# K and V of six batches as four rows on 128 partitions and a padded rest: linear attention and a gated MLP on one Trainium2 core

## The chip, the cores and the metric

The kernel runs on one core of one Trainium2 chip. The core has a matrix engine (TensorE; in the profile PE for matmuls and PEld for weight loads), a vector engine (VectorE, DVE), a scalar engine (ScalarE, ACT), a general engine (GpSimd, POOL) and a queue engine (SyncE, SP). Each takes its instructions in order. Here POOL issues the loads from memory, which also convert 32-bit to 16-bit floats, and SP issues the stores and the transposing transfers between tiles. The metric is device microseconds of one execution; lower is better.

## What is computed

Eight batches with eight heads each, 576 positions, 64 values per head. For each batch and head a 64x64 matrix is formed from K and V over all positions, Q is multiplied by it, and each row is normalized. The result, 4608 rows of 512, goes through two matrix products with a gate between them.

```python
def _attn_ref(q, k, v, g_norm) -> np.ndarray:
    kv = np.einsum('bhsd,bhse->bhde', k, v)
    out = np.einsum('bhsd,bhde->bhse', q, kv)
    rms = np.sqrt(np.mean(out * out, axis=-1, keepdims=True) + 1e-06)
    return (out / rms * g_norm).astype(np.float32)

def _moe_ref(x, w_in, w_out) -> np.ndarray:
    h = x @ w_in
    g = h * (1.0 / (1.0 + np.exp(-1.702 * h)))
    return (g @ w_out).astype(np.float32)
```

## The kernel before, in words

**Stages.** The loop over t (L925) has nine stages. Stage t puts 512 rows of batch t through the two products of the second half: the first with the gate (`hid_seven`, matmuls of L527; in stage 0 `first_columns` and L420), then the one with w_out (`Seven.run`, L647; in stage 0 `project_all`, L761). Stages 1 to 8 use seven products of half size in place of eight, with sums made on VectorE (xS, gS, ws and tw are such sums). The last stage takes the 64 remaining rows of each of the eight batches, gathered in `x_rem`.

**Attention runs one batch ahead.** In stage t the attention of batch t + 1 is put between the steps of the two products. The order is written by hand: `at1` and `at2` hang a piece of work behind a numbered step of the first or second product, and a Plan names the order of the first product's steps, "kv" among them. Instructions stand on each engine in the order in which the program makes them; semaphore waits between engines are added from the tiles that they read and write.

**K times V.** `kv(c)` handles a pair of heads. `kv_product` (L215) sums over positions: K is the weight and V the moving operand, 64 columns each, and the two heads of a pair write the two halves of the output partitions in turn. Positions lie as 96 partitions of six rows each (PE_ = 96, NJ = 6), so each head takes six matmuls, each pair 12, and each batch 48. Batch 0 runs them in stage 0's beginning, batch 1 in four pieces in the second half of stage 0 (steps 36, 37, 49 and 50), batches 2 to 7 in one piece of 48 at "kv" (`kv_all`). VectorE then copies the sum into kvb or kvd (L355, L477).

**Loads of K and V.** There is one buffer each, `kraw` and `vbuf`, so the loads of a batch wait until the product of the batch before has read them. `load_kv` (L107) makes one DMA for K and one for V, with 96 partitions and, per head, one run of six rows: 1536 bytes in memory. Batch 2 is loaded in stage 0 in two halves, behind steps 39 and 51; batch t + 2 is loaded in stage t behind "kv". On POOL's queue `load_q` follows (L116): q's first 512 positions as 128 partitions of four rows, 1024 bytes per run, and the 64 remaining ones as two DMAs into `qrem`, of 64 partitions and 256 bytes per run.

**What else uses the DMA engines.** Behind step 100 of stage t, SP transposes q of batch t + 2 into qTd and qTr (L242, L244). The normalized rows x of batch t + 1 are transposed into xT, which the next stage reads (`turn`, L316). SP also issues the stores of the results.

**Stage 0's end on VectorE.** Behind steps 49 to 62 stand the copies of batch 1's products, `apply` (L341), copies of the results (L770) and the first sums xS (L459) of stage 1.

Of the kernel before, what the change touches and what calls it, by code (L numbers as in the profile page):

```python
# [12 lines left out]
P = 128  # L13
# [3 lines left out]
def kernel(  # L17
# [10 lines left out]
    nc = tc.nc  # L28

    B, H, S, D = q.shape  # L30
    DM = H * D
    DFF = moe_w_in.shape[1]
    NPAIR = H // 2
# [3 lines left out]
    SM = 512  # L37
    J = SM // P
    R = S - SM
# [22 lines left out]
    srcs = {"k": k, "v": v, "q": q}  # L62
# [21 lines left out]
    raw = {"k": kraw, "q": qraw, "v": vbuf}  # L84

    def early_src(n, b, c0, c1):
        return srcs[n][b, 2 * c0 : 2 * c1].rearrange("h (p j) d -> p h (j d)", j=NJ)

    def early_load(n, b, c0, c1):
        nc.gpsimd.dma_start(  # L90
            out=raw[n][0:PE_, c0:c1, :].rearrange("p c (l x) -> p (c l) x", l=2),
            in_=early_src(n, b, c0, c1),
        )
# [10 lines left out]

    def load_kv(b, c0=0, c1=NPAIR):  # L107
        early_load("k", b, c0, c1)
        early_load("v", b, c0, c1)

    def q_rows(b):

# [16 lines left out]
    for n in "kqv":  # L129
# [11 lines left out]
        out=ident,  # L141
        in_=ident,
# [50 lines left out]
    class Attention:  # L193
        ss_pool = rest_pool = (ps_a, "att")
        KEEP = NPAIR

# [11 lines left out]
        def kv(self, c):  # L208
            if c % self.KEEP == 0:
                self.kvp = ps_a.tile([P, NPAIR, D], F32, name="kvp", tag="att")  # L210
            self.kv_product(self.kvp[:, c, :], c)
            if (c + 1) % self.KEEP == 0:
                self.keep_kv(c + 1 - self.KEEP, c + 1)

        def kv_product(self, t, c):  # L215
            for j in range(NJ):
                for hl in range(2):
                    x = slice((hl * NJ + j) * D, (hl * NJ + j + 1) * D)
                    nc.tensor.matmul(  # L219
                        t[hl * D : (hl + 1) * D, :],  # L220
                        kraw[0:PE_, c, x],
                        vbuf[0:PE_, c, x],
                        start=(j == 0),
                        stop=(j == NJ - 1),
                    )
# [6 lines left out]
        def keep_kv(self, c0, c1):  # L232

            for half in range(2):
                to = slice(half * D, (half + 1) * D)
                for hl in range(2):
                    r = slice(hl * D, (hl + 1) * D)
                    copy(self.engine, self.kb[to, c0:c1, half, 1 - hl], self.kvp[r, c0:c1, :])
# [109 lines left out]

    class Early(Attention):
        KEEP = 2  # L350

        def keep_kv(self, c0, c1):
            for hl in range(2):
# [370 lines left out]
    def layers(t, units1, units2):  # L724
        hid = d0 if t == 0 else Hidden(t)
        seven = Seven(t, hid.gT) if t else None
        left = hid_seven(t, hid, seven, units1) if t else first_columns(hid, units1)
        osbs[t] = opool.tile([P, 4, DM], F32, name="osb", tag="osb")
        if t:
            todo = {n: [lambda x=x: seven.sums(*x) for x in xs] for n, xs in plan(t).later.items()}  # L730
            for n, us in units2.items():
                todo.setdefault(n, []).extend(us)
            for n, us in left.items():
                todo[n] = us + todo.get(n, [])
            seven.run(todo)
        else:
            project_all(hid.gT, units2)
        if t < EARLY:
            store_early(t)
        elif t < B and t not in HALVED:  # L740
            store(t, 0, J)
# [174 lines left out]
    def plan(t):  # L916
        return SECOND if t < EARLY else LATER if t < B - 1 else LAST_TWO
# [7 lines left out]
    for t in range(NT):  # L925
        b = t + 1
        u1, u2 = {}, {}

        def at1(i, f, *args):
            u1.setdefault(i, []).append(lambda: f(*args))  # L930

        def at2(i, f, *args):
            u2.setdefault(i, []).append(lambda: f(*args))  # L933

        def of(b, name, *args):
            return lambda: getattr(live[b], name)(*args)

        if t == 0:
            for l in range(2):
                at1(6, nc.vector.memset, kvd[l], 0.0)  # L940
            at1(7, of(0, "out", NPAIR))
            at1(7, scale_w_in, 0, 4)
            at1(7, w_in_sums, 0, 2)
            at1(8, start, 1)
            at1(11, scale_w_in, 4, 6)
            at1(11, w_in_sums, 2, 3)
            at1(13, load_q, 2)
            at2(4, setattr, a0, "ss_pool", Attention.ss_pool)
            at2(4, of(0, "ss", NPAIR, True))
            at2(4, of(0, "apply", NPAIR))  # L950
            at2(18, weight_sum, 0, 0, HF)
            at2(18, scale_w_in, 6, 8)
            at2(18, w_in_sums, 3, 4)
            for c in range(NPAIR):
                at1(12, of(1, "pack_q", c))
                at2(9 + 3 * c, of(1, "q", c))
                at2((36, 37, 49, 50)[c], of(1, "kv", c))
                at2((41, 43, 54, 55)[c], of(1, "out", c))
                at2((45, 50, 58, 60)[c], of(1, "ss", c))
                at2((48, 52, 58, 62)[c], of(1, "apply", c))  # L960
            for n in range(1, 4):
                at2(19, weight_sum, n, 0, 4)
                at2(38, weight_sum, n, 4, 6)
            at2(39, load_kv, 2, 0, 2)
            at2(51, load_kv, 2, 2, NPAIR)

            def first_sum():
                made[1] = Sums(1, xT[1])
                made[1].form(0)

            at2(55, first_sum)
        elif b < B:
            todo = plan(t)
            at1(todo.steps.index("kv"), of(b, "kv_all", todo.keep))
            if t == 1:
                at1(5, start, b)
                at1(5, of(b, "transpose_q"))
                at1(4, nc.scalar.preload_act_table_set, "gelu_apprx_sigmoid_and_others")
                for n, i in ((1, 8), (2, 11), (3, 16)):
                    at1(i, weight_sum, n, 6, HF)  # L980
            if t + 2 < B:
                late = max(15, todo.steps.index("kv") + 1)
                at1(late, load_kv, t + 2)
                at1(late, load_q, t + 2)
                at2(100, start, t + 2)
                at2(100, of(t + 2, "transpose_q"))
            at = todo.attn
            at2(at["table"], nc.scalar.preload_act_table_set, "abs_reciprocal_sqrt_and_small")
            for h in range(2):
                at2(at["roots"][h], of(b, "roots", h))  # L990
            for j in range(J):
                for name in ("rows", "add_up", "turn"):
                    at2(at[name][j], of(b, name, j))
            at2(46, of(b, "out", NPAIR))
            at2(74, of(b, "ss", NPAIR))
            at2(80, of(b, "apply", NPAIR))
            at2(82, nc.scalar.preload_act_table_set, "gelu_apprx_sigmoid_and_others")
        elif t < B:
            for name in ("ss_pool", "rest_pool"):
                at2(16, setattr, live[1], name, (ps_a, "att"))  # L1000
            at2(16, of(1, "out", NPAIR))
            at2(34, nc.scalar.preload_act_table_set, "abs_reciprocal_sqrt_and_small")
            at2(44, of(1, "ss", NPAIR))
            at2(50, of(1, "apply", NPAIR))
            at2(52, nc.scalar.preload_act_table_set, "gelu_apprx_sigmoid_and_others")
        layers(t, u1, u2)
# [30 lines left out]
```

## Time and profile before

| | |
|---|---|
| median of three runs | 263.08 us (262.53 to 263.4) |
| the profiled execution | 262.59 us, span 260.8 us |
| TensorE busy | 252.9 us, 97% of the span, 2548 matmuls |
| TensorE weight loads busy | 207.0 us, 79% |
| VectorE busy | 194.2 us, 74% |
| ScalarE busy | 174.9 us, 67% |
| GpSimd busy | 44.1 us, 17% |
| granted TensorE clock | 1.0 throughout |
| loads issued by GpSimd | 28112 packets, 18.17 MB written |

The span reaches from the first to the last instruction; the rest of the execution's time lies around it. Matmuls are pipelined and their ends are modelled, so a busy TensorE says little by itself: the chain of work that ended last, and what TensorE waited for, say whether it is the bound. In the chain each row gives the start, the length, and the engine, tile and line, with the number of instructions merged. In the groups each row gives line, engine, operation, tiles, shapes and count, then the busy time and the mean duration of one, then the idle time before. In the rows of DMA issues the last number is the time from issue to landing, and KB are those written. In the stretches each engine's busy time is followed, in the single rows, by the instructions in brackets.

### The profile page before, as it was taken

The numbers are of one execution on the slowest core, as the hardware profiler recorded it, in microseconds if no ns is written. First come the engines' busy times: TensorE is split into PE (matmuls) and PEld (weight loads), VectorE is DVE, ScalarE is ACT, GpSimd is POOL, SyncE is SP. The second block draws the span as 40 slices with busy tenths as digits, with TensorE's granted clock in tenths as the row PEclk, the third lists the DMA queues.
The fourth block names the chain that finished last, engine by engine and source line by source line (L and its number), as shares of the span: only waits on it lengthen the run. The fifth ranks groups of instructions, "written<-read, shape, count | busy, mean of one in ns | idle before, by whom it ended". The sixth has DMA issues, their size and how long they took to land.

```text
span 260.8 us, 6238 instructions
## 1 busy us (share of the span) xinstructions
PE 252.9 (97%) x2548; PEld 207.0 (79%) x2548; DVE 194.2 (74%) x349; ACT 174.9 (67%) x315; POOL 44.1 (17%) x69
## 2 busy tenths in 40 slices
PE   7899999999999999999999999999999999999993
PEld 2444544788888988898889888998899888888882
DVE  1566676899968986899689958995899587466941
ACT  3477724988639963996399648974797569737810
POOL 8872234004023002300140004000000000000001
PEclk9999999999999999999999999999999999999999
DMA  7999999979979946995699369946600510021005
GB/s 175 194 202 205 205 204 197 246 162 144 190 153 189 203 71 161 117 240 78 159 150 234 53 158 149 237 54 155 155 1 13 157 77 0 3 101 63 1 3 161
DMA packets 59311, 35.33 MB, mean 135 GB/s; under 512 B 31570, under 2 KB 56658, under 8 KB 59154
## 3 DMA queue, kind: packets, MB, share of 16 engines
q0 software_dynamic: 28112, 18.17, 49.6%
q1 hardware_dynamic: 30768, 16.36, 26.2%
q8 instruction: 20, 0.33, 0.5%
q10 hardware_dynamic: 402, 0.39, 0.5%
q14 instruction: 9, 0.07, 0.1%
HBM read 36.70 MB, written 9.44 MB: 177 GB/s over the span
## 4 chain that ended last, share of the span: by engine, by line
PE 89%; DMA 6%; POOL 2%; issue 0%; DVE 0%
PE h L527 38%; PE o L647 38%; PE o L761 5%; DMA w_in_sb<-in_moe_w_in_dram 4%; PE kvp L219 2%; DMA qraw<-in_q_dram 2%; PE outR L279 2%; PE hT L420 2%; POOL w_in_sb L154 2%; PE ss L327 1%; PE q L401 0%; PE outT L252 0%; PE outT L256 0%; POOL vbuf L90 0%; DVE osb L627 0%
## 5 line engine op out<-in xcount | busy, mean ns | idle before, releaser
L507 ACT ACTIVATE gT<-h 128x512 f16<-128x512 f32 x96 | 52.7, 604 | 5.4 <-PE h L527 5.3
L527 PEld LDWEIGHTS <-ws 128*128 128x128 f16 x512 | 50.1, 98 | 5.9
L647 PEld LDWEIGHTS <-gS 128*128 128x128 f16 x512 | 49.7, 98 | 5.6
L527 PE MATMUL h<-xS,ws 128*128 128x256 f16 x384 | 52.2, 272 | 0.0
L647 PE MATMUL o<-tw,gS 128*128 128x256 f16 x384 | 46.3, 273 | 0.0
L527 PEld LDWEIGHTS <-w_in_sb 128*128 128x128 f16 x384 | 37.1, 98 | 4.7
L647 PEld LDWEIGHTS <-gT 128*128 128x128 f16 x384 | 37.0, 98 | 4.0
L647 PE MATMUL o<-w_out_sb,gT 128*128 128x256 f16 x256 | 33.5, 273 | 0.0
L527 PE MATMUL h<-xT,w_in_sb 128*128 128x256 f16 x224 | 31.9, 273 | 0.0
L541 DVE TENSOR_TENSOR h<-h,s 128x512 f32<-128x512 f32 x32 | 22.2, 698 | 7.7 <-PE h L527 5.9
L624 DVE TENSOR_TENSOR osb<-o,qf 128x512 f32<-128x512 f32 (+1 forms) x25 | 16.7, 668 | 15.0 <-PE o L647 12.3
L90 POOL DMA_DIRECT2D kraw<-in_k_dram x12 | 8.7, 724 | 103.9 <-PE kvp L219 101.4
L543 DVE TENSOR_TENSOR s<-h,s 128x512 f32<-128x512 f32 x32 | 22.1, 691 | 3.9 <-PE h L527 3.1
L579 DVE TENSOR_TENSOR gS<-gT 128x512 f16<-128x512 f16 (+2 forms) x32 | 21.6, 684 | 0.7 <-ACT gT L507 0.7
L507 ACT ACTIVATE gT<-s 128x512 f16<-128x512 f32 x32 | 19.8, 628 | 2.7 <-DVE s L543 2.6
L329 ACT ACTIVATE rs<-ss,eps_t 128x512 f32<-128x512 f32 (+1 forms) x16 | 9.2, 582 | 16.8 <-PE ss L327 16.7
L527 PE MATMUL h<-xS,w_in_sb 128*128 128x256 f16 x128 | 18.9, 273 | 0.0
L933 ACT ACT_TABLE_LOAD x14 | 18.0, 1283 | 0.3
L680 POOL DMA_DIRECT2D out_dram<-osb x2 | 1.1, 564 | 94.2 <-DVE osb L624 94.2
L477 ACT COPY h<-h 128x512 f32<-128x512 f32 x27 | 15.6, 585 | 2.1 <-PE h L527 2.0
L477 ACT COPY s<-h 128x512 f32<-128x512 f32 x18 | 10.6, 588 | 9.5 <-PE h L527 8.8
L527 PE MATMUL h<-xT,ws 128*128 128x256 f16 x112 | 16.8, 273 | 0.0
(92 smaller groups left out, 362.4 us busy)
## 6 DMA issues: line engine op xcount, KB each, us to landing
out_dram<-osb SPq DMA_DIRECT2D x10, 512.0 KB, 3.1
kraw<-in_k_dram POOLq DMA_DIRECT2D x5, 576.0 KB, 8.4
vbuf<-in_v_dram POOLq DMA_DIRECT2D x5, 576.0 KB, 11.6
qraw<-in_q_dram POOLq DMA_DIRECT2D x3, 512.0 KB, 13.5
qbuf<-in_q_dram POOLq DMA_DIRECT2D x3, 512.0 KB, 14.6
kraw<-in_k_dram POOLq DMA_DIRECT2D x4, 288.0 KB, 10.4
vbuf<-in_v_dram POOLq DMA_DIRECT2D x4, 288.0 KB, 10.6
out_dram<-osb SPq DMA_DIRECT2D x6, 192.0 KB, 5.0
```

The source lines that it names most:

```text
L90: nc.gpsimd.dma_start(out=raw[n][0:PE_, c0:c1, :].rearrange("p c (l x) -> p (c l) x", l=2), in_=early_src(n, b, c0, c1),)
L329: nc.scalar.activation(rs[:, 0:n], t[:, 0:n], AFT.Abs_reciprocal_sqrt, bias=eps_t, scale=1.0 / D)
L477: (nc.vector.tensor_copy if engine == "D" else nc.scalar.copy)(to, src)
L507: nc.scalar.activation(self.gT[:, to, n * TH : (n + 1) * TH], src, AFT.Gelu_apprx_sigmoid)
L527: nc.tensor.matmul(bank[name][:, a], w, x, start=(p in (1, 5) and a == 0 and k == 0), stop=(k == KH - 1), skip_group_check=True,)
L541: nc.vector.tensor_add(bank["z"], bank["x"], self.s5)
L543: nc.vector.tensor_add(self.s5, bank["x"], self.s5)
L579: op(s[:, n, lo], a, b)
L624: nc.vector.tensor_add(o, ps, self.kept[with_][:, m])
L647: nc.tensor.matmul(o, a, w, start=(p in (1, 2, 5) and i == 0 and (mo == 0 or split)), stop=(i == HF - 1), skip_group_check=True,)
L761: nc.tensor.matmul(os[mo], gT[:, fo, mo * P : (mo + 1) * P], w_out_sb[:, fo, :], start=(fo == 0), stop=(fo == FO - 1),)
L933: u2.setdefault(i, []).append(lambda: f(*args))
```

## The change

For batches 2 to 7 K and V are laid out as Q is. The first 512 positions stand on 128 partitions with four rows each; the 64 remaining positions stand behind them on partitions 0 to 63, one row each, at columns RS to RS + 512 of the same buffers, and partitions 64 to 127 of these columns are set to zero. The product takes five steps per head: four over the rows and one over the rest with all 128 partitions. `load_kv` makes four DMAs in place of two: K, V, rest of K, rest of V. In stage 0 the first two are made for four heads at step 39, without the rest; at step 51 come `clear_rest`, the other four heads and both rests. The zeros are written once, since later loads of the rest write partitions 0 to 63 alone. Batches 0 and 1 keep the old layout and the old product, as `early_kv_product`.

```diff
-    def load_kv(b, c0=0, c1=NPAIR):
-        early_load("k", b, c0, c1)
-        early_load("v", b, c0, c1)
+    kv_rows = {n: raw[n].rearrange("p c x -> p (c x)") for n in "kv"}
+    RW = J * D
+    RS = H * RW
+
+    def load_kv(b, h0=0, h1=H, rest=True):
+
+        for n in "kv":
+            nc.gpsimd.dma_start(
+                out=kv_rows[n][:, h0 * RW : h1 * RW].rearrange("p (h x) -> p h x", x=RW),
+                in_=srcs[n][b, h0:h1, 0:SM, :].rearrange("h (p j) d -> p h (j d)", j=J),
+            )
+        for n in "kv" if rest else "":
+            nc.gpsimd.dma_start(
+                out=kv_rows[n][0:R, RS : RS + H * D].rearrange("p (h d) -> p h d", d=D),
+                in_=srcs[n][b, :, SM:S, :].rearrange("h p d -> p h d"),
+            )
+
+    def clear_rest():
+        for n in "kv":
+            nc.vector.memset(kv_rows[n][R:P, RS : RS + H * D], 0.0)
...
         def kv_product(self, t, c):
+            for j in range(J + 1):
+                for hl in range(2):
+                    h = 2 * c + hl
+                    x = RS + h * D if j == J else h * RW + j * D
+                    nc.tensor.matmul(
+                        t[hl * D : (hl + 1) * D, :],
+                        kv_rows["k"][:, x : x + D],
+                        kv_rows["v"][:, x : x + D],
+                        start=(j == 0),
+                        stop=(j == J),
+                    )
+
+        def early_kv_product(self, t, c):
             for j in range(NJ):
...
     class Early(Attention):
         KEEP = 2
+        kv_product = Attention.early_kv_product
...
-            at2(39, load_kv, 2, 0, 2)
-            at2(51, load_kv, 2, 2, NPAIR)
+            at2(39, load_kv, 2, 0, H // 2, False)
+            at2(51, clear_rest)
+            at2(51, load_kv, 2, H // 2, H)
```

## Prediction

> **What bounds the kernel now.** I read the chain of work that ended last first, then its pieces in order of time, then TensorE's own waits, then the busy time by stretches.
>
> ```profile
> PE 89%; DMA 6%; POOL 2%; issue 0%; DVE 0%
> ```
>
> ```profile
> 56.91 0.88 PE kvp L219 x48
> ...
> 74.31 0.87 PE h L527 x8
> 75.19 0.88 PE kvp L219 x48
> 76.07 11.02 PE h L527 x100
> ...
> 181.42 0.88 PE kvp L219 x48
> ```
>
> ```profile
> PE idle L809 <- DVE one_t L175: 1.3, 1, 1.3
> ```
>
> ```profile
> PE hT L420 <- DMA w_in_sb<-in_moe_w_in_dram: 0.2, 1, 0.2
> ```
>
> ```profile
> sum 46.00, PE 46.00 PEld 41.12 DVE 38.82 ACT 32.52 POOL 7.43; mean PE 2.00 PEld 1.79 DVE 1.69 ACT 1.41 POOL 0.32
> ```
>
> The first fence is the page's chain: 89% of the span is TensorE following itself. The second is the chain in time (start, length, what): the K-times-V product of one batch is one piece of 48 matmuls, 0.88 us long, and six of them (batches 2 to 7, from 56.91 to 181.42) lie on the chain with a matmul directly before and after. The third and fourth hold the first and last of the only six waits that TensorE's matmuls show; all belong to the start, where inputs and weights arrive. The fifth sums 23 stretches of 2 us from 57 to 103: TensorE is busy in all 46 us, VectorE in 38.8, ScalarE in 32.5. So a matmul removed from one of the six pieces shortens the span by what it held TensorE, as long as nothing it hands to or takes from another engine or a DMA is late by more than its present slack.
>
> **The matmuls.** The new product has five steps per head in place of six: 40 matmuls per batch in place of 48, and 40 weight loads in place of 48. Batches 0 and 1 keep the old form. Removed: 8 x 6 = 48 pairs of instructions.
>
> ```profile
> 42.62 0.31 PE kvp L219 x12
> ```
>
> ```profile
> 93.55 0.12 PE outT L256 x4
> ```
>
> ```profile
> L219 PE MATMUL kvp<-vbuf,kraw 96*64 96x64 f16 x336 | 7.2, 197 | 0.0
> ...
> L401 PEld LDWEIGHTS <-qbuf 96*128 96x128 f16 x24 | 1.5, 97 | 0.9
> L256 PE MATMUL outT<-qTr,kvd 128*128 128x64 f16 x24 | 1.7, 193 | 0.0
> L327 PEld LDWEIGHTS <-ones 128*128 128x128 f16 x16 | 1.6, 98 | 0.8
> ```
>
> The length 0.88 / 48 = 18.3 ns is not the price of one more matmul, since each piece has a fixed part. Batch 1 runs the same product in pieces of 12, at 0.31 us. The 36 matmuls between 12 and 48 cost 0.88 - 0.31 = 0.57 us, which is 15.8 ns each and leaves 0.12 us fixed (entry and exit). Two heads write opposite halves of the output partitions, so a pair takes 32 ns, close to the 0.12 / 4 = 30 ns of a single 64-column matmul of L256. Per batch the removed eight are worth 8 x 15.8 = 0.126 us, over six batches **0.76 us**. If the fixed part shrank in proportion, which I see no reason for, it would be 8 x 6 x 18.3 = 0.88 us; that is the upper end.
>
> What remains gets taller: 128 rows in place of 96. No 128-row, 64-column weight load is in the trace, so I bound it. The low end is no change: a weight load takes 97 ns with 96 rows (L401) and 98 with 128 (L327), a 64-column matmul 197 ns with 96 rows (L219) and 193 with 128 (L256). The high end is a price that grows with the rows, 15.8 x 128/96 = 21.1 ns: 40 x 21.1 - 48 x 15.8 = +0.086 us per batch, +0.5 us in all. I take the low end, since two pairs of rows at these very row counts show nothing.
>
> On this the Trainium skill (TensorE: Matmul & The Clock Gate, LDWEIGHTS) says that a weight load is paid by its columns and not by its contraction rows; the L401 and L327 rows agree. The same page (Wait — 56ns, not 53.3ns?) states a floor of about 25 ns between matmul starts; the 15.8 ns here are below it, for matmuls that alternate between column halves, and by the floor the gain would be an estimated 48 x 25 = 1.2 us. The measurement decides.
>
> Each product gets one more pair of waits, at its first rest step, for the rest's loads. Batch 2 already has a second wait in the middle of its product, for its second pair of loads, and its piece is 0.88 us like the others: a wait that is already met costs nothing to see.
>
> **VectorE.** Two memsets are added at step 51 of stage 0, of 64x256 words each.
>
> ```profile
> L139 DVE MEMSET kvb<- 128x256 uint32 x1 | 0.3, 272 | 0.0
> ```
>
> ```profile
> 45.64 0.42 DVE L459 TENSOR_TENSOR xS<-xT 128x512 f16<-128x512 f16 x1
> 47.24 0.69 DVE L341 TENSOR_TENSOR xT<-outT,rs 128x512 f16<-128x512 f32 x1 [1.18 <-ACT rs L329]
> ```
>
> ```profile
> 47.98 0.60 PE L527 MATMUL h<-xS,ws 128*128 128x256 f16 x4
> ```
>
> Together 2 x 0.27 = 0.54 us, behind the copies that already wait for the same product. Queued behind them are an apply, a copy and the first sum xS; then VectorE sits idle 1.18 us until ScalarE's rs. The idle time takes the 0.54 us, and xS ends at 46.6 in place of 46.06, before its first reader at 47.98. Cost nothing; without that idle time it would be 0.54 us once. In the later stages VectorE has no new work, and the product's copies to kvd start when VectorE gets to them, so TensorE's lead there grows by 0.13 us against slacks that I see no wait in.
>
> **The loads.** Each of batches 3 to 7 now issues k, v, rest of k, rest of v, q and two qrem: seven DMAs on POOL's queue where five were, the two rests ahead of q. Batch 2 issues six in place of four. Bytes are the same; pieces are of 1024 source bytes in place of 1536, and the rests of 256.
>
> ```profile
> 58.09 0.78 POOL L90 DMA_DIRECT2D kraw<-in_k_dram  x1 [12.69 <-PE kvp L219]
> 58.87 0.77 POOL L90 DMA_DIRECT2D vbuf<-in_v_dram  x1
> 59.63 0.89 POOL L117 DMA_DIRECT2D qbuf<-in_q_dram  x1
> 60.51 1.25 POOL L123 DMA_DIRECT2D qrem<-in_q_dram  x2
> ```
>
> ```profile
> kraw<-in_k_dram POOLq DMA_DIRECT2D x1, 576.0 KB, 6.0
> vbuf<-in_v_dram POOLq DMA_DIRECT2D x1, 576.0 KB, 8.1
> qbuf<-in_q_dram POOLq DMA_DIRECT2D x1, 512.0 KB, 10.0
> qrem<-in_q_dram POOLq DMA_DIRECT2D x2, 32.0 KB, 9.2
> ```
>
> The issues are 2 x 0.62 us more of POOL, which has nothing else to do. Landing (issue plus the last column): k 64.1, v 67.0, q 69.6, the second qrem (issued 61.1) 70.3. So 576 KB in 96 partitions took 2.9 us (200 KB/us), the 512 KB of q, in 128 partitions and pieces of 1024 as k and v will be, 2.66 (192), and the two qrem, of the rests' very pieces, 64 KB in 0.65 (100). New: 1024/192 + 128/100 = 6.6 us for k and v against 5.8, so the batch ends **0.8 us later**, at about 71.1.
>
> What is late next? K and V of batch 3 are read at 75.19: about 7 us of slack. Closer are two transfers that share the DMA engines:
>
> ```profile
> 68.29 2.69 SPq L316 DMA_TRANSPOSE xT<-x  x2
> ```
>
> ```profile
> xT<-x SPq DMA_TRANSPOSE x1, 4.9
> ```
>
> ```profile
> 74.22 0.43 DVE L459 TENSOR_TENSOR xS<-xT 128x512 f16<-128x512 f16 x1 [0.92 <-DMA xT<-x]
> ```
>
> In stage 1 the first xT transpose, issued 68.29, lands at 73.2 and TensorE reads it at 74.31: 1.1 us. If it moves with the loads' end by the whole 0.8, it lands at 74.0; TensorE comes at 74.18 then. It holds, by 0.2 at most. VectorE's sum of the second half would be 0.8 later too, and is read five products on. Later stages have room:
>
> ```profile
> 104.47 0.89 POOL L117 DMA_DIRECT2D qbuf<-in_q_dram  x1
> ```
>
> ```profile
> qbuf<-in_q_dram POOLq DMA_DIRECT2D x1, 512.0 KB, 15.4
> ```
>
> ```profile
> 120.93 2.63 SPq L316 DMA_TRANSPOSE xT<-x  x2
> ```
>
> There q lands at 119.9 and the transposes at 120.93 follow it, with more than 3 us left at their end before the stage that reads them at 127.4. Batch 2 is read first, at 56.91:
>
> ```profile
> 44.07 0.67 POOL L90 DMA_DIRECT2D kraw<-in_k_dram  x1 [3.16 <-PE kvp L219]
> 44.73 0.67 POOL L90 DMA_DIRECT2D vbuf<-in_v_dram  x1
> ```
>
> ```profile
> kraw<-in_k_dram POOLq DMA_DIRECT2D x1, 288.0 KB, 7.1
> vbuf<-in_v_dram POOLq DMA_DIRECT2D x1, 288.0 KB, 9.1
> ```
>
> Its last load lands at 53.8, at 288 KB in 2.66 us (108 KB/us, shared with stage 0's stores). The 0.8 us become 0.8 x 200/108 = 1.5: 55.3, still 1.6 ahead of the product. So the loads cost nothing; the bounds are that and the case below.
>
> **Sum.** -0.76 (matmuls) + 0 (rows) + 0 (VectorE) + 0 (loads) = -0.76 us. The profiled execution took 262.59 us, 1.8 around its span of 260.8, and becomes 261.8; the median of the runs, 263.08, is 0.49 above it, so the forecast is **262.3**.
>
> **Rivals.**
> 1. *The rests are written by half of the DMA engines* (slower). Both lie in partitions 0 to 63, while the two qrem of the measured price fill both halves. If the partition picks the engine, 128 KB through one half cost four times the qrem pair, 2.6 us in place of 1.28. Stage 1's loads then end 0.8 + 1.3 = 2.1 us later, xT lands at 75.3 and TensorE waits 1.1; batch 2 ends at 55.3 + 1.3 x 200/108 = 57.7 and TensorE waits 0.8. Together +1.9 - 0.76 = +1.1: 264.2. It turns the sign once the rests cost about 2.2 us. Against it: loads of 96 partitions, which would fill the halves two to one, ran at 200 KB/us beside 192 for 128. The Trainium skill (DMA: Bandwidth & Descriptors, The descriptor swizzle) has such a map for a 128-partition load, partitions 0 to 63 to engines 0 to 7; no view here shows engines singly. Chance 0.14.
> 2. *The taller matmuls cost by their rows*: +0.5 us, 263.6. Against it the two pairs of rows above. Chance 0.05.
> 3. *xT is late in stage 1 by some tenths*: the 0.2 us that I leave is within my reading of the landings. A wait of 0.2 to 0.6 us once leaves -0.2 to -0.5: 262.7. For it: VectorE already waits 0.92 us for that transfer. Chance 0.20.
> 4. *The fixed part shrinks too*, or the eight were dearer than 15.8: -0.88 or a little more, 262.1. Chance 0.13.
>
> **How the numbers follow.** The forecast itself has the remaining 0.48, its own range 262.0 to 262.6. About 0.3% is 0.8 us, what a measurement of this kernel tells from no change (its three runs spread over 0.87); the forecast lies just inside, so half of it counts as faster and most of the rest as no change. Faster: 0.6 x 0.48 + all of rival 4 + a little of 3 = 0.45; slower: rival 1, half of 2, and some of a spread between sessions, 0.20; within: 0.35. The range runs from 261.6 (rival 4 with a session 0.5 us quicker) to 263.7, past rivals 2 and 3 and short of rival 1's end.
>
> **What would show it.** In the profile after, the six kvp pieces of the chain should be 40 long and 0.75 us, with the stage period 0.13 shorter; the 64-column weight load stays near 113 ns. TensorE should have no new wait. Rival 1 or 3 would show as a TensorE wait before the matmuls at 74.2 or the product at 56.9, on xT or on kraw or vbuf, and a late q in stage 1; rival 2 as kvp pieces of 0.97. I am wrong if a wait stands in stages 2 to 6, where I found only room, or if the pieces shorten and the span does not.

## The result and the profile after

| | before | changed | ratio of the runs, 95% interval |
|---|---|---|---|
| first measurement, 6 and 6 runs | 263.12 us | 261.96 us (261.36 to 262.08) | 0.9955 (0.9939 to 0.9972) |
| second measurement, beside other kernels, 23 and 12 runs | 262.71 us | 262.13 us | 0.9985 (0.9972 to 0.9998) |

The changed kernel is faster, by 0.15 to 0.45%. The forecast, 262.3 us with 0.76 us gained, is a ratio of 0.9971: it lies just inside the upper end of the first interval and just below the second, so the medians alone do not settle the size.

The chain of waits of the changed kernel, in order of time (start and length in us, what, instructions merged):

```profile
24.16 5.35 PE hT L451 x24
...
57.22 0.75 PE kvp L237 x40
...
75.38 0.75 PE kvp L237 x40
76.13 11.02 PE h L558 x100
...
181.10 0.75 PE kvp L237 x40
...
245.20 10.60 PE o L678 x97
```

and the two rows of the same view of the kernel before that belong beside its first and last:

```profile
23.85 5.35 PE hT L420 x24
...
245.70 10.60 PE o L647 x97
```

The product's line is L237 now, and its piece holds 40 matmuls in 0.75 us where 48 took 0.88. What lies between the pieces is as it was (11.02 us for the 100 matmuls behind each of the five later pieces, in both kernels). From the first piece to the last block of the kernel it is 245.20 - 57.22 = 187.98 us, where it was 245.70 - 56.91 = 188.79: **0.81 us less**, of which six times 0.13 is 0.78. TensorE's first long piece starts 0.31 us later in this execution, at 24.16, when w_in has arrived. What runs before that moment is the same in both, so the spans, 260.2 and 260.8, differ by less than the middle does. From there to the first kvp piece, the stretch that holds the new memsets and batch 2's loads, it is 33.06 us in both.

The groups of the changed kernel's product (line, engine, operation, tiles, shapes, count, then busy us and mean ns of one):

```profile
L237 PE MATMUL kvp<-vbuf,kraw 128*64 128x64 f16 x240 | 4.9, 197 | 0.0
...
L237 PEld LDWEIGHTS <-kraw 128*64 128x64 f16 x240 | 4.3, 112 | 1.3 <-issue 1.3
```

With 128 rows a matmul still takes 197 ns from start to end, and a weight load 112, as with 96.

The loads of batch 3 in the changed kernel, first POOL's issues in order of time, then the rows of these DMAs (KB written, us from issue to landing):

```profile
58.24 0.88 POOL L114 DMA_DIRECT2D kraw<-in_k_dram  x1 [11.61 <-PE kvp L237]
59.12 0.89 POOL L114 DMA_DIRECT2D vbuf<-in_v_dram  x1
60.09 0.69 POOL L119 DMA_DIRECT2D kraw<-in_k_dram  x1
60.78 0.69 POOL L119 DMA_DIRECT2D vbuf<-in_v_dram  x1
61.45 0.90 POOL L134 DMA_DIRECT2D qbuf<-in_q_dram  x1
```

```profile
vbuf<-in_v_dram POOLq DMA_DIRECT2D x1, 512.0 KB, 8.0
qbuf<-in_q_dram POOLq DMA_DIRECT2D x1, 512.0 KB, 9.3
kraw<-in_k_dram POOLq DMA_DIRECT2D x1, 64.0 KB, 7.5
vbuf<-in_v_dram POOLq DMA_DIRECT2D x1, 64.0 KB, 7.2
```

V lands at 67.1, the two rests at 67.6 and 68.0, q at 70.75. The 128 KB of the rests took 0.9 us behind V. Relative to the batch's first issue q lands at 12.5 us, where it was 11.5 (12.1 in the second profile of the changed kernel, e5_changed_again). Batch 2's last rest, issued at 45.95, takes 9.1 us and lands 2.2 us ahead of its product (forecast 1.6). What shares the engines with it, and who waits:

```profile
xT<-x SPq DMA_TRANSPOSE x1, 3.7
```

```profile
xT<-x SPq DMA_TRANSPOSE x1, 5.2
```

```profile
75.09 0.42 DVE L490 TENSOR_TENSOR xS<-xT 128x512 f16<-128x512 f16 x1 [1.59 <-DMA xT<-x]
```

The first xT transpose of stage 1, issued at 68.48, lands at 72.2; the second, issued some 1.3 us later, at about 75. VectorE now waits 1.59 us for the second, where it waited 0.92; the experiments find nearly the same without the new loads. TensorE shows no new wait. VectorE in stage 0:

```profile
44.71 0.27 DVE L126 MEMSET kraw<- 64x256 uint32 x1
44.99 0.27 DVE L126 MEMSET vbuf<- 64x256 uint32 x1
...
46.50 0.42 DVE L490 TENSOR_TENSOR xS<-xT 128x512 f16<-128x512 f16 x1
47.54 0.69 DVE L371 TENSOR_TENSOR xT<-outT,rs 128x512 f16<-128x512 f32 x1 [0.63 <-ACT rs L359]
```

The memsets are there at 0.27 us each, and the idle time ahead of the L371 at 47.54 is 0.63 us in place of 1.18: they lie in it.

### The profile page after: what moved, and what is told of

Same layout as the page of the kernel before. It is cut to its first block, busy times and chain, and to the rows that moved or that the text cites. A ratio compares the mean times of both kernels' runs of the same rounds, so it can differ in the third digit from the quotient of the medians.

```text
span 260.2 us, 6161 instructions
## 1 busy us (share of the span) xinstructions
PE 251.4 (97%) x2500; PEld 206.1 (79%) x2500; DVE 194.8 (75%) x351; ACT 174.8 (67%) x315; POOL 53.3 (20%) x81
## 4 chain that ended last, share of the span: by engine, by line
PE 89%; DMA 7%; POOL 2%; issue 0%; DVE 0%
PE h L558 38%; PE o L678 38%; PE o L792 5%; DMA w_in_sb<-in_moe_w_in_dram 4%; DMA qraw<-in_q_dram 2%; PE outR L309 2%; PE hT L451 2%; PE kvp L237 2%; POOL w_in_sb L171 2%; PE ss L357 1%; PE kvp L249 0%; PE q L432 0%; PE outT L282 0%; PE outT L286 0%; POOL vbuf L90 0%
## 5 line engine op out<-in xcount | busy, mean ns | idle before, releaser
L114 POOL DMA_DIRECT2D kraw<-in_k_dram x7 | 6.0, 853 | 93.0 <-PE kvp L237 87.9
L792 PE MATMUL o<-w_out_sb,gT 128*128 128x512 f16 x64 | 16.6, 380 | 0.0
```

The costliest lines, as they stand in the source:

```text
L114: nc.gpsimd.dma_start(out=kv_rows[n][:, h0 * RW : h1 * RW].rearrange("p (h x) -> p h x", x=RW), in_=srcs[n][b, h0:h1, 0:SM, :].rearrange(" ...
L792: nc.tensor.matmul(os[mo], gT[:, fo, mo * P : (mo + 1) * P], w_out_sb[:, fo, :], start=(fo == 0), stop=(fo == FO - 1),)
```

## The experiments

Eight kernels were measured, e1 to e4 on one chip and e5 to e8 on another, each group beside the kernel before (medians 262.72 and 262.71 us). The column "middle" is the time from the first kvp piece to the last block of 97 matmuls, taken from each kernel's chain as above; the start of the program, which varies from execution to execution, is not in it.

| run | kvp piece | middle | median | ratio, 95% interval |
|---|---|---|---|---|
| before | 0.88 x48 | 188.79 | | |
| changed | 0.75 x40 | 187.98 | | |
| e1_five_old | 0.75 x40 | 188.02 | 262.03 | 0.9972 (0.9952 to 0.9992) |
| e2_six_new | 0.88 x48 | 188.74 | 263.16 | 1.0018 (0.9998 to 1.0037) |
| e3_unpadded | 1.57 x40 | 192.92 | 267.30 | 1.0171 (1.0145 to 1.0196) |
| e4_rest_twice | 0.75 x40 | 188.81 | 262.79 | 1.0001 (0.9979 to 1.0023) |
| e5_changed_again | 0.75 x40 | 187.99 | 262.13 | 0.9985 (0.9972 to 0.9998) |
| e6_double_product | 1.39 x80 | 191.78 | 265.86 | 1.0127 (1.0112 to 1.0143) |
| e7_unpadded_last | 0.87 x40 | 188.72 | 262.80 | 1.0005 (0.9991 to 1.0018) |
| e8_merged | 0.75 x40 | 187.98 | 261.69 | 0.9966 (0.9952 to 0.9979) |

**Five steps in the old layout.**

```diff
-            for j in range(NJ):
+            nj = NJ if self.b < EARLY else NJ - 1
+            for j in range(nj):
...
-                        stop=(j == NJ - 1),
+                        stop=(j == nj - 1),
```

> The kernel before with its old layout, loads and no memsets, but five steps per head in place of six in batches 2 to 7: the sixth row of each partition of K and V is left out of the product. Theory (only the number of matmuls pays, 15.8 ns each): kvp pieces of 40 at 0.75 us, 0.76 us less than before, ratio 0.9971. Rival (the new layout and its loads pay some 0.4 us of the 1.16 measured): the same 0.76, so the changed kernel at 0.9955 stays clearly below this one. Rival (the matmuls are worth 1.16 us, 24 ns each): ratio 0.9956 and pieces of 0.69.

This kernel leaves a sixth of the positions out of the sums of batches 2 to 7, so it serves for its time alone. The ratio is 0.9972 and the piece is 0.75 us, in the chain of this kernel:

```profile
56.95 0.75 PE kvp L220 x40
```

Matmuls of 96 rows, with the old loads, give what the change gives: the same piece, and a middle of 188.02 against 187.98. The number of matmuls accounts for the gain, and the new layout and its loads for nothing that these traces show. The third case (24 ns each) falls.

**Six steps in the new layout.** The sixth step multiplies by a tile of zeros, and `stop` moves to it.

```diff
+    zero = const.tile([P, D], F16)
...
-            for j in range(J + 1):
+            for j in range(J + 2):
...
-                        kv_rows["k"][:, x : x + D],
+                        zero if j > J else kv_rows["k"][:, x : x + D],
...
```

> The changed kernel with a sixth step per head, whose weights are a tile of zeros: 48 matmuls per batch again, all with 128 rows, loads and memsets as changed. Theory: the rows cost nothing, kvp pieces of 48 at 0.88 us, time of the kernel before, ratio 1.000. Rival (price by rows): pieces of about 1.13 us, ratio 1.006. Rival (layout and loads pay 0.4 us by themselves): pieces of 0.88 and ratio 0.9985.

The chain of this kernel:

```profile
56.55 0.88 PE kvp L239 x48
```

The piece of 48 is 0.88 us with 128 rows as with 96, and the middle is 188.74 against 188.79. The 32 rows more cost nothing. The ratio, 1.0018, has 1.000 inside its interval, which reaches from 0.9998 to 1.0037, and the piece decides.

These two kernels also bear on the transposes of stage 1. VectorE's first sum, which starts when the second xT transpose has landed, in e1_five_old (old loads, 40 matmuls) and in e2_six_new (new loads, 48):

```profile
74.59 0.42 DVE L460 TENSOR_TENSOR xS<-xT 128x512 f16<-128x512 f16 x1 [1.39 <-DMA xT<-x]
```

```profile
73.83 0.43 DVE L492 TENSOR_TENSOR xS<-xT 128x512 f16<-128x512 f16 x1 [0.88 <-DMA xT<-x]
```

Counted from its own first kvp piece the sum starts at 17.64 us in e1_five_old and 17.28 in e2_six_new; it was 17.31 in the kernel before, and is 17.87 and 17.63 in the two profiles of the changed kernel. The first transpose lands 3.2 us after its issue in e1_five_old and 4.9 in e2_six_new, against 4.9 before and 3.7 and 3.5 in the changed kernel. So the shift is there without the new loads and absent with them; some 0.2 us, as much as the changed kernel's own two profiles differ by, is what the loads can have added. Nor is it the length of the piece: e7_unpadded_last, below, has the shift too (3.4 and 17.78 us), with a piece of 0.87 us. What moves these transposes stays open.

**The rest on 64 partitions, without zeros.**

```diff
+                    r = slice(0, R if j == J else P)
...
-                        kv_rows["k"][:, x : x + D],
-                        kv_rows["v"][:, x : x + D],
+                        kv_rows["k"][r, x : x + D],
+                        kv_rows["v"][r, x : x + D],
...
-            at2(51, clear_rest)
```

> The changed kernel with the rest's step on 64 partitions alone, and without the two memsets of zeros. Theory: the price of a matmul does not depend on its rows, so pieces of 40 at 0.75 us and the changed kernel's time, ratio 0.9955 to 0.997. Rival (a matmul on half of the rows between full ones costs a change of the array's arrangement, twice per pair of heads, 8 per batch): pieces longer by 8 times 30 ns or more, 1.0 us or more, ratio 1.001 or more.

Two views of this kernel, the chain and the product's line in one stage:

```profile
103.52 1.57 PE kvp L238 x40
```

```profile
L238 PEld LDWEIGHTS <-kraw x40: 102/109/113, 103.5 to 104.9; 128*64 128x64 f16 x32, 64*64 64x64 f16 x8
```

The theory fell and the other case held: a piece of the same 40 matmuls is 0.82 us longer, and the kernel 1.7% slower than before. The weight loads themselves are no longer (109 ns in the middle, the eight of 64 rows among them), so the time lies between the instructions. Inside the piece the rows change seven times, 128 to 64 four times and back three times: 0.82 / 7 = 0.117 us each, if the changes are what costs; the next experiment tells. Without the zeros the change would not pay in this order of steps.

**The rests' steps last.** The same without zeros, with all row steps ahead of all rest steps.

```diff
...
-            for c in range(NPAIR):
-                self.kv(c)
+            self.kvp = ps_a.tile([P, NPAIR, D], F32, name="kvp", tag="att")
+            for steps in (range(J), (J,)):
+                for c in range(NPAIR):
+                    self.kv_product(self.kvp[:, c, :], c, steps)
+            self.keep_kv(0, NPAIR)
```

> The kernel without padding once more (rest on 64 partitions, no memsets), with the four row steps of all pairs first and the rest's steps of all pairs behind them: two changes between 128 and 64 rows per batch in place of eight. The order in which the sums accumulate is changed with it. Theory (each change of rows costs about 0.1 us, the 0.82 us by which the unpadded pieces were longer over eight): pieces of about 0.95 us, ratio about 1.0015. Rival (the 64-row matmul itself is dear): pieces of 1.57 us as before, ratio 1.017.

```profile
103.06 0.87 PE kvp L238 x40
```

That is the chain of this kernel: 0.87 us, 0.12 over the padded piece. The expectation counted two changes; there is one inside the piece, since leaving it is a change in every form, and nothing more shows behind it: the middle is 0.74 us over the changed kernel's, six times 0.12. The two unpadded kernels differ by six changes and by 1.57 - 0.87 = 0.70 us, 0.117 each again, and one more change accounts for the 0.12: the 64-row matmuls themselves cost no more. The Trainium skill (TensorEngine Tiling (Array Packing), Key Properties) says that a change of the tiling mode drains TensorE. If a step from 128 to 64 rows is such a change, these two runs agree, at 0.12 us each; no view here shows the draining itself.

**Each rest loaded twice.**

```diff
...
+            nc.gpsimd.dma_start(
+                out=spare[n][0:R], in_=srcs[n][b, :, SM:S, :].rearrange("h p d -> p h d")
+            )
```

> The changed kernel with each rest of K and V loaded a second time, into a tile that nobody reads: 128 KB more per batch, the suspected transfer doubled. Theory: the rests took 0.45 us per 64 KB in the changed kernel, so stage 1's loads end 0.9 us later; the second xT transpose, at 75.0 in the changed kernel, lands at about 75.9, VectorE's first sum in stage 2 is late by that, and TensorE waits up to 0.5 us once; ratio 0.996 to 0.998. Rival (that transfer is hidden with more room): ratio as the changed kernel, 0.9955, and no wait on TensorE. Rival (loads bound the kernel in every stage): 5 us or more longer.

The chain of this kernel leaves TensorE in stage 1, and TensorE's timeline shows two waits in stage 2 that the changed kernel does not have:

```profile
69.55 6.57 DMA xT<-x
```

```profile
76.69 1.53 PE L562 MATMUL h<-xS,ws 128*128 128x256 f16 x12 [0.27 <-DVE xS L494]
78.06 1.04 PE L562 MATMUL h<-xT,w_in_sb 128*128 128x256 f16 x8
79.26 1.05 PE L562 MATMUL h<-xS,ws 128*128 128x256 f16 x8 [0.17 <-DVE kvd L512]
```

The second transpose lands at 76.1; counted from its own execution's first kvp piece (56.97, and 57.22 in the changed kernel) that is 1.4 us later than in the changed kernel, where 0.9 was expected. TensorE waits first for the sum made from it, and then for VectorE's copies to kvd, which stand behind that sum. The waits in brackets count from the modelled ends of the matmuls ahead; by their starts these three rows are held up by 0.44, 0.06 and 0.32 us against the changed kernel's. The middle is 0.83 us longer (188.81 against 187.98), more than the 0.5 expected, which counted the first wait alone, and the ratio, 1.0001, lies above the 0.996 to 0.998 expected. The direction and the place are as expected; the gain of the change is gone. So 128 KB more in stage 1 is enough to end the gain, and the later stages, each with the same added loads, show nothing.

**The changed kernel again.** No edit.

> The changed kernel as it is, measured a second time, since its first ratio (0.9955, interval 0.9939 to 0.9972) lies 0.4 us beyond the 0.76 us that its pieces account for. Theory (the pieces are the whole gain, the rest was the spread between executions): kvp pieces 0.75 us and ratio near 0.997. Rival (a second gain of 0.4 us outside the pieces): ratio near 0.9955 again.

0.9985, with pieces of 0.75 and a middle of 187.99. A second gain of 0.4 us is not found: this interval excludes 0.9955, as the first one excludes 0.9985, and both touch 0.9972. What made the first measurement larger and the second smaller than the 0.8 us of the middle was not settled; the middle itself repeats within 0.01 us.

**The product twice.**

```diff
-            for j in range(J + 1):
+            for j in [*range(J + 1), *range(J + 1)]:
```

> The changed kernel with every product of batches 2 to 7 done twice, the second over the first: 80 matmuls per batch in place of 40. Theory (0.12 us fixed and 15.8 ns each): pieces of 80 at 1.38 us, 3.8 us more than the changed kernel, ratio about 1.0115 against the kernel before. Rival (18.3 ns each, nothing fixed): 4.4 us more, pieces of 1.47. Rival (24 ns, as the measured 1.16 us would ask): 5.8 us more, ratio 1.019.

The chain of this kernel:

```profile
103.38 1.39 PE kvp L237 x80
```

0.12 + 80 x 0.0158 = 1.384 us was expected, 1.38 to 1.39 is there, and the middle is 3.80 us longer than the changed kernel's. The price of one more matmul is 15.8 ns, and a fixed part belongs to each piece.

**Batch 1's pieces joined.**

```diff
-                at2((36, 37, 49, 50)[c], of(1, "kv", c))
+                at2((37, 37, 50, 50)[c], of(1, "kv", c))
```

> The changed kernel with batch 1's four pieces of 12 joined to two of 24, by moving the first and third behind the step of the second and fourth. Theory (each entry into 64-column matmuls has 0.12 us fixed): pieces of 24 at 0.50 us in place of 2 x 0.31, 0.24 us less, ratio 0.0009 below the changed kernel. Rival (the steps behind them wait for the pair that now comes later): the gain is lost to a wait in stage 0.

The chain of e5_changed_again at that place, and that of e8_merged:

```profile
35.07 3.89 PE o L792 x18
38.96 0.31 PE kvp L249 x12
39.26 0.32 PE o L792
39.59 0.31 PE kvp L249 x12
39.90 0.97 PE o L792 x4
```

```profile
34.98 4.10 PE o L792 x19
39.08 0.50 PE kvp L249 x24
39.58 0.97 PE o L792 x4
...
47.78 9.21 PE h L558 x84
```

A piece of 24 takes 0.50 us in place of twice 0.31, and the matmul that stood alone between the two took 0.32 us, where those ahead of the piece take 0.22 each (3.89 us for 18); moved there, it adds 0.21. So a joined pair saves about 0.12 us in the product and about 0.1 in the matmul behind it. The long pieces have the same: the 100 matmuls of h behind a kvp piece take 11.02 us, and the 100 that start at 206.66 in the changed kernel, with no kvp piece ahead of them, 10.92. From the first long piece (24.47 and 24.38) to stage 1's first, 48.33 in e5_changed_again, it is 23.40 us in place of 23.86: 0.46 us for two joined pairs, twice what was expected. No wait took it back. On the same chip the joined version is at 261.69 us against the changed kernel's 262.13, and its ratio of 0.9966 (0.9952 to 0.9979) makes it faster than the kernel before; its lead over the changed kernel rests on the trace, as their intervals overlap.

## Why the prediction was right

- **The price of the matmuls** was the whole forecast and held: 15.8 ns each from the difference between pieces of 12 and 48, 0.75 us forecast for a piece of 40 and 0.75 found, 0.81 us less in the middle for a forecast 0.76. e6_double_product found the same price with twice the number. Dividing a piece by its count, 18.3 ns, would have been wrong, as the fixed part stays. The 25 ns per matmul, by which the prediction worked out 1.2 us beside its sum, would have left pieces of 0.68 us.
- **The rows** cost nothing between 96 and 128, as taken: e2_six_new shows 0.88 us for 48 matmuls of 128 rows. Rival 2 falls.
- **VectorE's memsets** lie in the idle time named, which shrank by 0.55 us for a forecast 0.54.
- **The loads** end later by about the amount forecast, 0.8 us for the batch's end: relative to the first issue K and V are complete 0.9 us later (0.75 in e5_changed_again) and q lands 1.0 later (0.6 there). The split was off: the rests took 0.9 us and not 1.28, and the rows of K and V, forecast 0.43 us shorter than before, ended 8.9 us after the first issue as before (8.6 in e5_changed_again).
- **Rival 1** (half of the DMA engines) falls. Its price was 2.6 us, and 0.9 is there. If half of the engines had written the rests, the other half should have gone on with q. From 66.5 to 67.0 us, while the rests run, the changed kernel's trace has 532 packets of loads, 496 of them under 512 bytes. In as long a stretch of q alone (67.2 to 67.7 in the kernel before) there are 194, none under 512 bytes; half of that would be 97, and 36 are there.
- **xT in stage 1** was the right place to look, but its step from the loads' end to xT did not come about. The prediction had the first transpose land at 74.0, with 0.2 us left for TensorE. It landed at 72.2, earlier than before; the second moved, from about 74.2 to 75.0, and e1_five_old shows most of that move with the old loads. That xT cost nothing was forecast, so the sum holds, but not for the reason given; there it was lucky. What was left behind the second transpose the prediction did not size; e4_rest_twice did: 1.4 us later (1.6 against e5_changed_again) costs 0.83 us, so an estimated 0.5 to 0.8 was left if the rest passes on one for one.
- **The 0.9955 of the first measurement** is more than the forecast's term, as 0.9985 is less. The traces have no second term (e1_five_old, e5_changed_again), and the term that they show is the forecast's. How close a single median comes to 262.3 is in part chance; the pieces and the middle are what bears the forecast out.

## What to carry to other kernels

Price a removed instruction from the difference between two lengths of the same sequence, not from its mean: entering such a sequence has its own price, which removing instructions leaves in place and joining sequences removes. Where TensorE is busy from end to end, zeros that keep the shape of all its matmuls the same can be cheaper than leaving the work out. Look for the transfer that will be late next among those that share the DMA engines with a changed load, not only at the load's own reader. And before a shift in the trace is put down to one part of a change, look for it in a kernel that has that part alone.

## What the runs showed of the hardware that was not expected

- A change from 128 to 64 contraction rows between 64-column matmuls costs 0.12 us of TensorE (0.82 us for seven changes, 0.12 for one), while the matmuls themselves cost the same.
- Entering and leaving matmuls with weights of 64 columns, between others of 128, costs about 0.23 us in all, half of it in the matmul behind the piece: 0.46 us for two entries saved. Matmuls of 64 moving columns with weights of 128 do not show it: four of L256 take 0.12 us in all.
- The two transposes of a pair in stage 1 moved in opposite directions from kernel to kernel. In the kernel before and in e2_six_new the first landed 4.9 us after its issue, and the sum behind the second started 17.3 us after the first kvp piece; in the changed kernel (both profiles), e1_five_old and e8_merged it was 3.2 to 3.7 and 17.6 to 17.9. The layout of the loads does not decide it, and the cause is open. Doubling the rests' loads delayed both, to 5.5 and 6.6 us after their issue (3.7 and 5.2 in the changed kernel).
